# A new opening for attention followed by a max-out MoE layer: V of batches 0 and 1 by hardware queue, weights in another order, M early, nine spans of 512 tokens

## The chip, the cores and the metric

The kernel runs on one core of one Trainium2 chip. The metric is the device time of one execution in microseconds (us); the time before is the median of three runs. The core has five engines with a queue of instructions each, executed in order: PE (matmul; its weight loads are listed as PEld), DVE (VectorE), ACT (ScalarE), POOL (GpSimd) and SP (SyncE, which here only starts DMA transfers). Engines wait for each other through semaphores. SP's and ACT's transfers go through hardware queues, Pool's through a software queue.

## The reference

Block-causal attention (8 batches, 8 heads, 576 tokens, head dimension 64, blocks of 64), then a layer on its output:

```
scores = q @ k.T / 8, masked where block(query) < block(key)
attn   = softmax(scores);  x = (attn @ v), heads side by side: 4608 tokens x 512
g      = maximum(x @ w1, x @ w2)          # w1, w2: 512 x 1024
out    = g @ w_out                        # w_out: 1024 x 512, result float32
```

All inputs are fp32; the kernel computes in bf16 with fp32 sums.

## The kernel before, in words

**The algebra.** max(a, b) = max(a - b, 0) + b. So the kernel forms d = w1 - w2 (`diff_w`, lines 160 to 162, DVE), g = max(x @ d, 0) (`h_unit`, lines 202 to 221), and M = w2 @ w_out (512 x 512, `m_unit`, lines 234 to 244, from w2 transposed by `bT_unit`, lines 223 to 232). Then out = x @ M + g @ w_out (`y_unit`, lines 252 to 264): 4 matmuls with M and 8 with w_out for a tile of 128 tokens.

**Attention.** A pair is two heads of one batch; there are 32 pairs, four a batch, and a group g is two pairs (16 groups). `load_qk` (line 112) brings q and k of a group (589,824 bytes each) into one of three raw buffers; with `gated` a one-element memset on Pool stands ahead, so that SP's transfer starts no earlier than Pool reaches it. `cast` (line 126) makes bf16, `transposes` (line 346) turns it on PE and copies PSUM to qT, kT. Scores are computed transposed (keys on partitions), go through two PSUM buffers (`ps_s`, bufs=2), and `exp` (line 394, ACT) writes them to aT. `mask` (line 399, Pool memsets) clears what causality forbids. `av` (line 463) multiplies aT by V, which carries a column of ones, so that DVE can divide by the row sums (lines 485, 486) into xp. `x_out` (line 503) transposes xp on PE into xT; for groups 4 to 14 `x_dma` does it by DMA. Pairs 0 to 3 (batch 0) are written as four bursts each (`burst_p`, `burst_q1`, `burst_q2`, `burst_q3`: 768, 1024, 1024 and 384 columns), pairs from 4 on as three tiles (`tile_0` to `tile_2`). A burst or tile needs the `ps_s` buffer of the one before last, hence the end of its exp.

V comes by `load_v` (line 134): a Pool (software) DMA that casts to bf16, five chunks of up to 128 keys a batch. w1, w2 and w_out come by Pool DMAs too, w2 and w_out cast on the way: w1 and w2 in four blocks of 256 columns, w_out in two halves. w2 rests in a part of xT that later batches overwrite.

**The order of the work** is written out by hand (`manual_schedule`): each engine executes what is emitted for it in the order of the code. Matmuls of the layer are filler: `plan` (line 285) lists units (h, bT, M, y), each with the token count it needs and a cost per matmul (1.0 for 512 columns, 0.5 for M, 0.25 for bT), and `fill(n)` (line 322) emits the next ready ones up to cost n. `fill_of(g)` (line 534) shares what is ready among the groups until the next batch's tokens are done.

Lines 578 to 680 are the opening. Warm-ups (`warm_up`, line 338) are matmuls on zeros. Batch 0's bursts are interleaved with the first `diff_w`, h and bT; q and k of group 2 arrive, and the tiles of pairs 4 and 5 (`region`, lines 657 to 667) follow at once, beside h; M and the first y units come after these. From line 682 the loop over groups 3 to 15 runs regions, fills, `av_with` of the pair two back, and `pool_work` (line 541), which emits on Pool the gated loads three groups ahead, the casts of q and k two groups ahead (`cast("q", 4)` and `cast("k", 4)` at s = 5), and `load_v` of the next batch.

The layer goes by spans of tokens. `spans` (lines 71, 72) are 256, 320, then 512 each, last 448; since a span may end inside a tile of 128 tokens, `carry` (line 76) counts the tokens handed to the next span, and `h_unit` copies their g on Pool (line 207).

Of the kernel before, what the change touches and what calls it, by code (L numbers as in the profile page):

```python
# [8 lines left out]
FP32 = mybir.dt.float32  # L9
BF16 = mybir.dt.bfloat16  # L10
# [4 lines left out]
def kernel(  # L15
# [55 lines left out]
    spans = [(0, QCUT), (QCUT, S - QCUT)]  # L71
    spans += [(t0, min(SPAN, NTOK - t0)) for t0 in range(S, NTOK, SPAN)]
    NSPAN = len(spans)


    carry = [t0 % P for t0, _ in spans]
    tiles = [(carry[i] + w) // P for i, (_, w) in enumerate(spans)]
# [62 lines left out]

    w1r = moe_w1.rearrange("(c p) f -> p c f", p=P)
# [4 lines left out]
    w1_raw, w2_sb = {}, []  # L146
    for j in range(d_ff // WB):
        row, n = (1, j) if j < 3 else (3, 0)
        t0 = 3 * S - 3 * BLK + n * NDM * WB
        w2_sb.append(xT[:, row, t0:t0 + NDM * WB].rearrange("p (c f) -> p c f", c=NDM))  # L150

    def load_w(j, which=(0, 1)):
        fs = slice(j * WB, (j + 1) * WB)
        if 0 in which:
            w1_raw[j] = wraw.tile([P, NDM, WB], FP32, name="w1raw")
            nc.gpsimd.dma_start(out=w1_raw[j][:], in_=w1r[:, :, fs])
        if 1 in which:
            nc.gpsimd.dma_start(out=w2_sb[j], in_=w2r[:, :, fs])

    def diff_w(j):  # L160
        fs = slice(j * WB, (j + 1) * WB)
        nc.vector.tensor_sub(d_sb[:, :, fs], w1_raw[j][:], w2_sb[j])  # L162
# [17 lines left out]
    load_qk(2, (SP, None))  # L180
# [10 lines left out]
    for c in range(2):  # L191
        load_v(0, c)
    load_w(0, (0,))
    cast("q", 1, ((pool, 7, RPP),))
    cast("k", 1, ((pool, 0, 7),))
    load_w(0, (1,))


# [3 lines left out]
    def h_unit(i, f):  # L202
        if f == 0:
            g_tiles[i] = g_pool.tile([P, NFF, SPAN + BLK], BF16, name="g")
            if carry[i]:
                end = carry[i - 1] + spans[i - 1][1]
                nc.gpsimd.tensor_copy(  # L207
                    out=g_tiles[i][:, :, :carry[i]],
                    in_=g_tiles[i - 1][:, :, end - carry[i]:end])
        g = g_tiles[i]  # L210
        t0, w = spans[i]
        m = carry[i]
        pt = ps_m.tile([P, SPAN], FP32, name="ps_h", tag="m")
        for c in range(NDM):
            nc.tensor.matmul(  # L215
                pt[:, :w], d_sb[:, c, f * P:(f + 1) * P], xT[:, c, t0:t0 + w],
                start=(c == 0), stop=(c == NDM - 1),
            )
            if c == NDM - 1:
                nc.vector.tensor_scalar_max(g[:, f, m:m + w], pt[:, :w], 0.0)  # L220
            yield

    def bT_unit(j):
        pt = ps_m.tile([P, 2, NDM, P], BF16, name="ps_bT", tag="m")
        for i in range(2):
            for c in range(NDM):
                nc.tensor.transpose(pt[:, i, c, :], w2_sb[j][:, c, i * P:(i + 1) * P], ident[:])
                if i == 1 and c == NDM - 1:
                    (act if j % 2 else dve)(
                        out=bT_sb[:, 2 * j:2 * j + 2, :],  # L230
                        in_=pt.rearrange("p i c d -> p i (c d)"))
                yield

    def m_unit(i, c):
        ds = slice(i * WH, (i + 1) * WH)
        pt = ps_m.tile([P, WH], FP32, name="ps_M", tag="m")
        for f in range(NFF):
            nc.tensor.matmul(  # L238
                pt[:], bT_sb[:, f, c * P:(c + 1) * P], wo_sb[:, f, ds],
                start=(f == 0), stop=(f == NFF - 1),  # L240
            )
            if f == NFF - 1:
                nc.vector.tensor_copy(out=m_sb[:, c, ds], in_=pt[:])
            yield

    def y_terms(i, s):
        g = g_tiles[i]
        t0 = spans[i][0] - carry[i] + s * P
        return [(xT[:, c, t0:t0 + P], m_sb[:, c]) for c in range(NDM)] + [
            (g[:, f, s * P:(s + 1) * P], wo_sb[:, f]) for f in range(NFF)]  # L250

    def y_unit(i, s):
        t0 = spans[i][0] - carry[i] + s * P
        py = ps_m.tile([P, d_model], FP32, name="ps_y", tag="m")
        terms = y_terms(i, s)
        for n, (lhs, rhs) in enumerate(terms):
            nc.tensor.matmul(  # L257
                py[:], lhs, rhs, start=(n == 0), stop=(n == len(terms) - 1),
            )
            if n == len(terms) - 1:  # L260
                y = y_pool.tile([P, d_model], FP32, name="y")
                (dve if i < 2 else act)(out=y[:], in_=py[:])  # L262
                nc.sync.dma_start(out=out[t0:t0 + P, :], in_=y[:])
            yield

    def y_last(i, s):
        t0 = spans[i][0] - carry[i] + s * P
# [17 lines left out]
    def plan():  # L285
        def h(i, f):
            t0, w = spans[i]
            units.append((h_unit(i, f), t0 + w, w / SPAN, NDM))

        def y(i, s, last=False):  # L290
            t0, w = spans[i]
            if last:
                units.append((y_last(i, s), t0 + w, 0.333, 3 * NY))
            else:
                units.append((y_unit(i, s), t0 + w, 1.0, NY))

        for i in range(NSPAN):
            for f in range(NFF):
                h(i, f)
                if i == 0 and f % 2:  # L300
                    units.append((bT_unit(f // 2), 0, 0.25, 2 * NDM))
                if i > 2 and f % 2 == 0 and f // 2 < tiles[i - 1]:
                    y(i - 1, f // 2)
            if i == 1:
                for n in range(2 * NDM):
                    units.append((m_unit(n // NDM, n % NDM), 0, 0.5, NFF))
                for j in range(2):
                    for s in range(tiles[j]):
                        y(j, s)
        n = tiles[-1]  # L310
        for s in range(n):
            y(NSPAN - 1, s, s == n - 1)

# [88 lines left out]
    def burst(p, parts, a0):  # L402
        u = ps_s.tile([P, 2, 512], FP32, name="ps_s", tag="s")
        w = 0
        for c, q0, n in parts:
            scores(p, u, w, c, q0, n)
            w += n
        exp(p, u, w, a0)

    def burst_p(p):  # L410
        burst(p, ((0, 0, QCUT), (1, P, QCUT - P)), 0)

    def burst_q1(p):
        burst(p, ((0, QCUT, 320), (1, QCUT, 192)), 384)

    def burst_q2(p):
        burst(p, ((1, 448, P), (2, QCUT, 320), (4, 512, BLK)), 896)

    def burst_q3(p):
        burst(p, ((3, 384, 192),), 1408)  # L420

    def masks_p(p, eng=None):
        for a in (0, 256):
            mask(p, a, eng)
# [116 lines left out]
    def pool_work(s):  # L541
        g, i = divmod(s, 2)
        if s == 4:
            load_qk(4, (SP, SP), gated=True)
# [31 lines left out]
    LOW = (0, -(-QCUT // RPP))  # L576
    HIGH = (LOW[1], NP)
# [9 lines left out]
    burst_p(0)  # L587
    masks_p(0)
# [3 lines left out]
    for c in range(2, NCH):  # L592
        load_v(0, c)
    load_qk(2, (None, SP), gated=True)
    load_w(1)
    cq = transposes("q", 1, (dve, dve))
    burst_q1(0)
    ck = transposes("k", 1, (dve, dve))
    for i in range(2):
        cq((i,), LOW)  # L600
        ck((i,), LOW)
    cq((0,), HIGH, act)
    cq((1,), HIGH, act)
    warm_up(3)
    burst_p(2)
    ck((0,), HIGH, dve)
    ck((1,), HIGH, dve)
    av(0, [0, 1])
    warm_up(2)
    burst_p(3)  # L610
    av(1, [0, 1])
    masks_p(2, nc.vector)
    burst_q3(0)
    masks_p(3, nc.vector)
    burst_q2(0)
    av(2, [0, 1])
    warm_up(2)
    x_out(0, 0, 2, (act, act))
    av(3, [0, 1])
    diff_w(0)  # L620
    burst_q1(1)
    warm_up(2)
    cast("q", 2, ((pool, 0, RPP),))
    masks_q(0)
    load_w(2)
    burst_q2(1)
    x_out(1, 0, 2)
    warm_up(2)
    burst_q3(1)
    masks_q(1)  # L630
    load_w(3)
    fill(4)
    burst_q1(2)
    transposes("q", 2, (dve, act))()
    burst_q2(2)
    av(0, [2, 3, 4])
    burst_q3(2)
    masks_q(2)
    cast("k", 2, ((pool, 0, RPP),))
    load_wo(0)  # L640
    load_wo(1)
    av(1, [2, 3, 4])
    burst_q1(3)
    burst_q2(3)
    av(2, [2, 3, 4])
    transposes("k", 2, (dve, act))()
    burst_q3(3)
    masks_q(3)
    pad_keys(4)
    pad_keys(5)  # L650
    load_qk(3, (SP, SP), gated=True)
    for c in range(NCH):
        load_v(1, c)
    x_out(0, 2, NCH)
    diff_w(1)
    fill(2)
    outs = tile_0(4), tile_1(4)
    av(3, [2, 3, 4])
    region(*outs)
    fill(2)  # L660
    diff_w(2)
    fill(4)
    x_out(1, 2, NCH)
    region(tile_2(4), tile_0(5))
    diff_w(3)
    fill(6)
    region(tile_1(5), tile_2(5))
    fill(6)
    cast("q", 3, ((pool, 0, RPP),))
# [88 lines left out]
```

The softmax here doesn't subtract the row's maximum and nothing guards it: scores larger than these inputs give would overflow.

## Time and profile before

| what | us |
|---|---|
| median of three runs (258.4 to 258.81) | 258.6 |
| the profiled execution's own time | 260.0 |
| its span, first to last instruction | 258.2 |
| PE busy | 247.4 |
| ACT busy / DVE busy / POOL busy | 143.2 / 136.1 / 110.4 |
| exps of batch 0 (16 bursts) | from 8.9 to 26.0 |
| exps of pairs 4 and 5 | from 26.7 to 34.4 |
| first scores of pair 6 (group 3 starts) | 42.2 |
| x_out(2) on PE (group 4 starts) | 55.2 |
| x_out(3) on PE (group 5 starts) | 66.3 |
| last matmul ends | 255.1 |

Times within the span count from its start. A row of groups gives the line, the engine, the operation, the output and input tiles with their shapes, the count, then the busy time and the mean ns of one, then the engine's idle time just before them and what ended most of it. In rows of the timeline the first two numbers are start and duration.

### The profile page before, as it was taken

How to read it: one execution, taken by the hardware profiler on the slowest of the kernel's cores; microseconds unless marked ns; L12 is line 12 of the kernel's file. 1: busy time of each engine (PE TensorE's matmuls, PEld its weight loads, DVE VectorE, ACT ScalarE, POOL GpSimd, SP SyncE). 2: the span in 40 equal slices, each digit the busy share in tenths (PEclk: the TensorE clock that was granted, in tenths of full speed). 3: DMA queues.
4: the chain of work that ended last, by engine and by line, in shares of the span. 5: the costliest groups of instructions: out<-in, count | busy, mean ns of one | idle time of the engine just before them, and what ended most of it. 6: DMA issues, size and time to landing. Idle time of an engine off the chain costs nothing.

```text
span 258.2 us, 7195 instructions
## 1 busy us (share of the span) xinstructions
PE 247.4 (96%) x2983; PEld 139.1 (54%) x2983; DVE 136.1 (53%) x299; ACT 143.2 (55%) x200; POOL 110.4 (43%) x274
## 2 busy tenths in 40 slices
PE   7598899799999999999999999999999999999995
PEld 2346678646555555555555554546464655444444
DVE  4967986556584428451845184518550853443200
ACT  2798854476574857586757665766576431000111
POOL 1987950584637263726382638163813010000000
PEclk9999999999999999999999999999999999999999
DMA  6999999499569995998599949985977122202122
GB/s 244 316 206 307 217 251 246 156 102 253 129 162 257 144 188 135 245 154 225 114 244 143 186 145 224 168 196 141 91 109 110 44 56 80 83 0 81 43 104 99
DMA packets 71265, 41.30 MB, mean 160 GB/s; under 512 B 53568, under 2 KB 58048, under 8 KB 71232
## 3 DMA queue, kind: packets, MB, share of 16 engines
q1 hardware_dynamic: 28544, 31.27, 43.4%
q0 software_dynamic: 42272, 8.92, 39.9%
q10 hardware_dynamic: 416, 0.66, 0.7%
q8 instruction: 23, 0.38, 0.6%
q14 instruction: 10, 0.08, 0.1%
HBM read 34.60 MB, written 9.44 MB: 171 GB/s over the span
## 4 chain that ended last, share of the span: by engine, by line
PE 84%; DMA 8%; POOL 3%; ACT 2%; issue 1%; DVE 0%; SPq 0%; POOLq 0%; ACTq 0%
PE ps_y L257 36%; PE ps_h L215 22%; PE ps_o L479 10%; PE ps_s L371 8%; DMA qraw<-in_q_dram 5%; DMA kraw<-in_k_dram 3%; PE ps_qT L352 2%; PE ps_kT L352 2%; PE ps_w L341 1%; ACT aT L395 1%; PE ps_y L272 1%; PE ps_M L238 1%; POOL kn L132 1%; PE ps_s L389 1%; ACT qT L360 1%
## 5 line engine op out<-in xcount | busy, mean ns | idle before, releaser
L395 ACT ACTIVATE aT<-ps_s 128x1024 bf16<-128x1024 f32 (+2 forms) x100 | 95.8, 996 | 25.8 <-PE ps_s L371 24.2
L257 PE MATMUL ps_y<-wo_sb,g 128*128 128x512 bf16 x280 | 69.8, 379 | 0.0
L215 PE MATMUL ps_h<-xT,d_sb 128*128 128x512 bf16 (+3 forms) x320 | 69.2, 358 | 0.3 <-DVE d_sb L162 0.3
L220 DVE TENSOR_SCALAR g<-ps_h 128x512 bf16<-128x512 f32 (+3 forms) x80 | 50.7, 636 | 30.6 <-PE ps_h L215 28.8
L400 POOL MEMSET aT<- 64x128 bf16 x124 | 22.4, 200 | 81.8 <-ACT aT L395 81.2
L485 DVE RECIPROCAL rec<-ps_o 128x4 f32<-128x4 f32 (+1 forms) x64 | 12.1, 188 | 62.5 <-PE ps_o L479 61.7
L215 PEld LDWEIGHTS <-d_sb 128*128 128x128 bf16 x320 | 29.0, 98 | 29.1 <-issue 2.7
L479 PEld LDWEIGHTS <-aT 128*128 128x128 bf16 x960 | 37.2, 98 | 13.5 <-issue 0.8
L262 ACT COPY y<-ps_y 128x512 f32<-128x512 f32 x31 | 18.2, 587 | 44.5 <-PE ps_y L257 36.1
L257 PEld LDWEIGHTS <-g 128*128 128x128 bf16 x280 | 25.8, 98 | 29.8 <-issue 2.0
L479 PE MATMUL ps_o<-vv,aT 128*128 128x65 bf16 x960 | 39.8, 194 | 0.0
L257 PE MATMUL ps_y<-m_sb,xT 128*128 128x512 bf16 x140 | 38.2, 380 | 0.0
L136 POOL DMA_DIRECT2D vv<-in_v_dram x40 | 33.7, 848 | 1.6 <-issue 1.2
L371 PE MATMUL ps_s<-qT,kT 64*128 64x64 bf16 (+6 forms) x344 | 31.2, 280 | 1.6 <-ACT kT L360 0.7
L486 DVE TENSOR_TENSOR xp<-ps_o,rec 128x256 bf16<-128x256 f32 (+1 forms) x64 | 31.4, 491 | 2.2
L360 ACT COPY qT<-ps_qT 128x576 bf16<-128x576 bf16 (+1 forms) x17 | 10.3, 614 | 19.9 <-PE ps_qT L352 19.9
L132 POOL CAST qn<-qraw 128x1152 bf16<-128x1152 f32 (+1 forms) x16 | 16.9, 1058 | 9.1 <-DMA qraw<-in_q_dram 9.1
L257 PEld LDWEIGHTS <-xT 128*128 128x128 bf16 x140 | 12.2, 98 | 15.1 <-issue 3.5
L371 PEld LDWEIGHTS <-kT 64*128 64x128 bf16 x344 | 12.3, 94 | 11.0 <-issue 6.2
L132 POOL CAST kn<-kraw 128x1152 bf16<-128x1152 f32 (+1 forms) x15 | 17.1, 1140 | 1.4 <-DMA kraw<-in_k_dram 1.4
L360 ACT COPY kT<-ps_kT 128x576 bf16<-128x576 bf16 x15 | 9.6, 639 | 14.4 <-PE ps_kT L352 14.4
L207 POOL COPY g<-g 128x512 bf16<-128x512 bf16 x8 | 4.9, 614 | 20.7 <-DVE g L220 20.3
(58 smaller groups left out, 161.8 us busy)
## 6 DMA issues: line engine op xcount, KB each, us to landing
qraw<-in_q_dram SPq DMA_DIRECT2D x16, 576.0 KB, 5.0
out_dram<-y SPq DMA_DIRECT2D x35, 256.0 KB, 3.7
kraw<-in_k_dram SPq DMA_DIRECT2D x15, 576.0 KB, 5.8
vv<-in_v_dram POOLq DMA_DIRECT2D x32, 128.0 KB, 5.7
w1raw<-in_moe_w_dram POOLq DMA_DIRECT2D x4, 512.0 KB, 8.1
xT<-in_moe_w_dram POOLq DMA_DIRECT2D x4, 256.0 KB, 8.6
wo_sb<-in_moe_w_out_dram POOLq DMA_DIRECT2D x2, 512.0 KB, 10.0
kraw<-in_k_dram ACTq DMA_DIRECT2D x1, 576.0 KB, 5.6
```

The source lines that it names most:

```text
L132: copy(out=n[:, j0:j1], in_=t[:, j0:j1])
L136: nc.gpsimd.dma_start(out=vv_r[b % NV][P - rows:, c, :, :D], in_=v[b, :, c * P:c * P + rows, :].rearrange("h p d -> p h d"),)
L215: nc.tensor.matmul(pt[:, :w], d_sb[:, c, f * P:(f + 1) * P], xT[:, c, t0:t0 + w], start=(c == 0), stop=(c == NDM - 1),)
L220: nc.vector.tensor_scalar_max(g[:, f, m:m + w], pt[:, :w], 0.0)
L257: nc.tensor.matmul(py[:], lhs, rhs, start=(n == 0), stop=(n == len(terms) - 1),)
L262: (dve if i < 2 else act)(out=y[:], in_=py[:])
L360: (copy or copies[i])(out=t[:, p0 * RPP:p1 * RPP].rearrange("q (p j) -> q p j", j=RPP), in_=pts[i][:, :, p0:p1].rearrange("q j p -> q p j"),)
L371: nc.tensor.matmul(ps[:, hh, col:col + w], kT[r, k0:k0 + P], qT[r, q0:q0 + w], start=True, stop=True,)
L395: nc.scalar.activation(out=aT_r[p % NA][:, :, a0:a0 + w], in_=ps[:, :, :w], func=AF.Exp, scale=scale,)
L400: (eng or nc.gpsimd).memset(aT_r[p % NA][BLK:, :, a0:a0 + BLK], 0.0)
L479: nc.tensor.matmul(po[:, gi, hh, :], a[:, hh, a0:a0 + P], vv[:, c, h0 + 2 * hh, :], start=(mm == 0), stop=(mm == n_mm - 1),)
L486: nc.vector.tensor_mul(xp[:, :, ts[0]:ts[0] + n, p % 2].rearrange("q s t d -> q t s d"), po[:, :, :, :D], rec[:, :n].to_broadcast([P, n, 2 ...
```

## The change

1. `stage_v(b, c)` loads a chunk of V as fp32 by SP into a free part of xT, `cast_v` copies it to bf16 (Pool). Batch 0 is staged right after q and k of group 1, where before q of group 2 was loaded; batch 1 after the loads of groups 2 and 3. Batches 2 to 7 keep `load_v`.
2. w2 is loaded in two halves (behind the casts of q1 and of k1 on Pool), then w_out in two halves, then w1 in four blocks.
3. Batch 0's four pairs run pair by pair (all bursts of pair 0, then pair 1, then 2 and 3), with warm-ups inside the bursts; bT and M are planned first and fill the later bursts; h follows once batch 0 is done; the loads of q and k for groups 2, 3 and 4 are gated behind batch 0's last masks, and the tiles of pairs 4 and 5 come after most of h of span 0.
4. Spans are nine times 512 tokens; the carry is gone.
5. Some PSUM copies change engine.

```diff
-    spans = [(0, QCUT), (QCUT, S - QCUT)]
-    spans += [(t0, min(SPAN, NTOK - t0)) for t0 in range(S, NTOK, SPAN)]
-    NSPAN = len(spans)
-    carry = [t0 % P for t0, _ in spans]
-    tiles = [(carry[i] + w) // P for i, (_, w) in enumerate(spans)]
+    NSPAN = NTOK // SPAN
+    NT_SPAN = SPAN // P
...
+    def v_stage(c):
+        row, n = (0, c) if c < 3 else (2, c - 3)
+        t0 = 3 * S - 3 * BLK + n * 2 * H * D
+        return xT[:, row, t0:t0 + 2 * H * D].bitcast(FP32).rearrange("p (h d) -> p h d", h=H)
+    def stage_v(b, c):
+        rows = min(P, S - c * P)
+        nc.sync.dma_start(
+            out=v_stage(c)[P - rows:],
+            in_=v[b, :, c * P:c * P + rows, :].rearrange("h p d -> p h d"),
+        )
+    def cast_v(b, c, copy):
+        rows = min(P, S - c * P)
+        copy(out=vv_r[b % NV][P - rows:, c, :, :D], in_=v_stage(c)[P - rows:])
...
+    def load_w2(i):
+        nc.gpsimd.dma_start(out=w2_sb[i], in_=w2r[:, :, i * WC:(i + 1) * WC])
...
-    load_qk(2, (SP, None))
+    for c in range(NCH):
+        stage_v(0, c)
...
-    for c in range(2):
-        load_v(0, c)
-    load_w(0, (0,))
     cast("q", 1, ((pool, 7, RPP),))
+    load_w2(0)
     cast("k", 1, ((pool, 0, 7),))
-    load_w(0, (1,))
...
 def bT_unit:
-                    (act if j % 2 else dve)(
+                    nc.vector.tensor_copy(
 def m_unit:
-                nc.vector.tensor_copy(out=m_sb[:, c, ds], in_=pt[:])
+                (act if i else dve)(out=m_sb[:, c, ds], in_=pt[:])
 def y_unit:
-                (dve if i < 2 else act)(out=y[:], in_=py[:])
+                (dve if i < 1 else act)(out=y[:], in_=py[:])
...
 def burst(p, parts, a0, warm=0):
         u = ps_s.tile([P, 2, 512], FP32, name="ps_s", tag="s")
         w = 0
+        for _ in range(warm):
+            nc.tensor.matmul(u[:, 0], zeros[:, :P], zeros[:], start=True, stop=True)
...
 def pool_work(s):
         if s == 4:
-            load_qk(4, (SP, SP), gated=True)
+            for c in range(NCH):
+                cast_v(1, c, pool)
```

The opening after the change, from the first burst on (one line holds several statements of the code):

```
burst_p(0); load_w2(1); masks_p(0); burst_p(1); warm_up(2); masks_p(1)
for c in range(3): cast_v(0, c, pool)
load_wo(0); transposes("q", 1, (dve, dve))(); burst_q1(0); transposes("k", 1, (dve, dve))()
burst_q2(0, 2); burst_q3(0, 2); masks_q(0)
for c in range(3, NCH): cast_v(0, c, pool)
load_wo(1); load_w1(0); load_w1(1)
burst_q1(1, 2); burst_q2(1, 2); av(0, [0, 1]); burst_q3(1, 2); masks_q(1); fill(2)
burst_p(2, 1); av(0, [2, 3, 4]); burst_p(3); masks_p(2); masks_p(3); fill(2)
av(1, [0, 1]); burst_q1(2); av(1, [2, 3, 4]); burst_q2(2); x_out(0); fill(4)
burst_q3(2); masks_q(2); load_w1(2); load_w1(3); av(2, [0, 1]); burst_q1(3, 1)
av(3, [0, 1]); burst_q2(3, 1); fill(4); burst_q3(3); masks_q(3); fill(4)
for g in (2, 3): load_qk(g, (SP, SP), gated=True)
for c in range(NCH): stage_v(1, c)
load_qk(4, (SP, SP), gated=True)
av(2, [2, 3, 4]); fill(4); av(3, [2, 3, 4]); fill(4); x_out(1, 0, NCH, (act, act))
diff_w(0); fill(8); cast("q", 2, ((pool, 0, RPP),)); diff_w(1); fill(8)
cast("k", 2, ((pool, 0, RPP),)); fill(8); diff_w(2); fill(8)
transposes("q", 2, (dve, act))(); diff_w(3); fill(8); transposes("k", 2, (dve, act))()
pad_keys(4); pad_keys(5); fill(5); region(tile_0(4), tile_1(4)); fill(6)
region(tile_2(4), tile_0(5)); fill(6); cast("q", 3, ((pool, 0, RPP),))
region(tile_1(5), tile_2(5)); fill(6); cast("k", 3, ((pool, 0, RPP),))
```

What follows (the rest of group 2, and the loop over groups 3 to 15) is unchanged in its text.

## Prediction, made before the changed kernel was run

> **What bounds the kernel now.** I read the page first, then the busy time by stretches, then the groups, then the timeline of the first 70 us. The page:
>
> ```profile
> span 258.2 us, 7195 instructions
> ...
> PE 247.4 (96%) x2983; PEld 139.1 (54%) x2983; DVE 136.1 (53%) x299; ACT 143.2 (55%) x200; POOL 110.4 (43%) x274
> ...
> PE   7598899799999999999999999999999999999995
> ...
> ACT  2798854476574857586757665766576431000111
> POOL 1987950584637263726382638163813010000000
> ...
> DMA  6999999499569995998599949985977122202122
> ```
>
> PE is full from about slice 9 (55 us) on; only the opening and the tail have room. I cut the opening where the work changes: first transposes (7.0), end of batch 0's exps (26.1), first scores of pair 6 (42.2), start of group 5 (66.3). The columns are the window, its length, and the busy time of PE, PEld, DVE, ACT, POOL.
>
> ```profile
> 7.00:26.10 19.10, 15.75 (x323) 9.94 (x323) 14.89 (x38) 16.08 (x25) 16.57 (x30) 1.00 1.43 273
> 26.10:42.20 16.10, 15.34 (x209) 11.49 (x208) 14.03 (x29) 9.57 (x12) 9.93 (x28) 1.00 1.66 217
> 42.20:66.30 24.10, 22.48 (x348) 14.55 (x347) 13.25 (x31) 15.11 (x20) 12.19 (x33) 1.00 0.87 182
> 66.30:240.00 173.70, 173.70 (x2001) 93.10 (x2001) 88.07 (x182) 96.85 (x135) 69.90 (x181) 1.00 0.77 143
> ```
>
> Busy PE time hides slow pace, so I price PE work by the distance between starts of successive matmuls in the full stretch: 216 ns for 512 columns (h, y), 109 for 256 (M), 56 for bT, 29 for av, 14.5 for a transpose; 0.85 us for a pair's scores. At these prices the useful work, warm-ups not counted, is 8.7 us from 7.0 to 26.1, 15.5 up to 42.2, 22.2 up to 66.3. So the three stretches lose 10.4, 0.6 and 1.9 us (together 12.9); later almost nothing. **The question is whether the new order loses less than 12.9 us before the same state is reached.**
>
> The other prices, from the groups:
>
> ```profile
> L395 ACT ACTIVATE aT<-ps_s 128x1024 bf16<-128x1024 f32 (+2 forms) x100 | 95.8, 996 | 25.8 <-PE ps_s L371 24.2
> L136 POOL DMA_DIRECT2D vv<-in_v_dram x40 | 33.7, 848 | 1.6 <-issue 1.2
> L132 POOL CAST qn<-qraw 128x1152 bf16<-128x1152 f32 (+1 forms) x16 | 16.9, 1058 | 9.1 <-DMA qraw<-in_q_dram 9.1
> ```
>
> And the one long stall after 42 us, PE behind Pool's cast of q4, itself waiting for its load:
>
> ```profile
> 46.18 1.15 POOL L132 CAST qn<-qraw 128x1152 bf16<-128x1152 f32 x1 [3.89 <-DMA qraw<-in_q_dram]
> 47.38 0.44 PE L352 MATMUL ps_qT<-ident,qn 64*128 64x64 bf16 x18 [1.61 <-POOL qn L132]
> ```
>
> **The Trainium skill.** "TensorE: Matmul & The Clock Gate", Back-to-back issue gap, gives N/2.4 + 2.5 ns: 216 ns for 512 columns, as the trace has it. "DMA: Bandwidth & Descriptors", SWDGE vs HWDGE vs iDMA: a transfer that casts must come from GpSimd; so V by a hardware queue lands as fp32 and needs a cast. Same page, Why small descriptors are slow: a 256-byte piece takes 11 cycles instead of 8. "GPSIMD Engine Reference", Engine selection: one-input copies run near line rate; here 256 columns took 0.41 us and 1152 took 1.14, so 0.2 us + 0.81 ns a column.
>
> **The change, part by part.**
>
> *V by hardware queue.* Ten software issues (V of batches 0, 1), about 0.85 us each, 8.4 us, leave Pool's queue. Ten casts of 512 columns come: 0.2 + 512 x 0.81 ns = 0.62 us each, 6.2 us. Loading: by software a chunk is 1024 packets, and the packet records show some 1100 of them per us: 0.95 us. By hardware no row shows it: if it keeps the 2048-byte pace (84 ns a packet, 16 engines) 0.67 us; at the 256-byte packets' mean of the later transposes (32 ns) 2.0 us; the skill's 11/8 on the weights' 374 GB/s gives an estimate of 0.96. I take 0.96: chunks land from 10.5 to about 14.5 us, sharing with w2. A gain against software isn't excluded, but k1, ahead in that queue, lands at 9.3 in any case.
>
> *Weights.* Order w2, w_out, w1, 2.1 MB each; now 128 packets of 4096 bytes (0.52 MB of w1) take about 1.4 us, so 5.7 us for each. Behind V that fills the DMA engines to about 30 us: w2 by 18 to 19, w_out 24, w1 30. q2 (gated behind batch 0's last masks, 27 us) lands near 32, k2 33, q3, k3 36, V of batch 1 41, q4, k4 44. SP's eleven issues from 27 on take 0.4 to 1.0 us each and are out before the first y store queues behind them (46 us). None of the loads is late for its user below except perhaps w2's first half (bT at 15.5, landing 15 to 16.5: 0 to 1 us).
>
> *Batch 0's bursts.* Each waits for the PSUM buffer of the burst before last; where two warm-ups stand ahead, release to next exp costs 0.05 + 0.43 + 0.38 + 0.04 = 0.9 us, hidden behind a 1.02 us exp, not behind one of 0.5. Exps start at 8.94 as now; they are 4 x (0.78 + 1.02 + 1.02 + 0.5) = 13.3 us. Gaps: 0.3 up to q3 of pair 0; 0.4 each behind the short q3s and where av, bT or M stand between (six places, 2.3); 1.6 where x_out(0) waits for DVE and two bT units follow it. Sum 4.2: end at 8.94 + 13.3 + 4.2 = 26.4, against 26.03 now. Pool just keeps up: masks to 11.6, three casts to 13.5, w_out's issue, masks, two casts to 16.0; av(0) of the late tiles wants them at 16.5. The four masks moved from DVE to Pool (0.8 us) and the 13 burst warm-ups (against 13 before) lie in waits: nothing; were av(0) late, each us would be one of the end.
>
> *M, then h, ahead of pairs 4 and 5.* After 26.4, PE ends M1 at 26.7 and then has av (1.8), M2 to M7 (48 x 109 ns, 5.2), x_out(1) (0.5), 29 matmuls of h (6.3) and q2's and k2's transposes (0.7): 41.2, with latencies 41.4. Copies that change engine (x_out(1) and half of M to ACT, bT and x_out(0) to DVE) fall where that engine waits; y copies stay 4 on DVE. PE is full, loses nothing. At 42.0 useful work done is 24.5 of 35, lost 10.5; before had lost 11.0 by 42.2. **A draw so far.** But pairs 4 and 5 had their six exps between 26.7 and 34.4 before; now ACT stands without exps from 26.4 to 41.8. And of batch 0's 120 filler units 87 are planned before group 3, instead of 56 of 124.
>
> *Groups 2 to 4 without filler.* From 41.8 ACT owes pairs 4 to 9: 18 exps x 0.98 + 6 x 0.27 + 6 copies of qT/kT x 0.64 = 23.1 us; PE only 21.0 (scores 5.1, av 3.6, transposes 1.6, x_out 1.0, 45 units 9.7). Walking on: pairs 4, 5 keep ACT to 48.4. Pool meanwhile does q3's cast, masks, k3's cast to 49.95, and then the five casts of V, **3.1 us that its queue puts ahead of pad_keys(6, 7) and of q4's and k4's casts**: pads to 54.1, q4 55.3, k4 56.4. Transposes of k3 at 50.3, copies to 51.0, first exp of pair 6 at 51.5 (ACT without work for some 2.5 us). Its third tile is issued behind q4's transposes: PE waits 54.0 to 55.3, and ACT from 53.5 to 55.7. Then each region costs ACT's 2.7 to 3 us plus small gaps: group 4 starts at 59.8 (8 or 9 units of filler), its q5 cast is awaited 0.2 us, group 5 starts at 68.8. PE did 21.0 of 26.8: lost 5.8.
>
> *Nine spans.* Same columns: 32 x (109 + 136 + 189) ns = 13.9 us become 64 x 216 = 13.8. Eight Pool copies (4.9 us) go, on nobody's path. But at group 5 span 0 covers 512 tokens instead of 576: four matmuls more remain, 0.9 us.
>
> **Sum.** 68.8 - 66.3 + 0.9 = +3.4 us; or by losses: 10.5 + 5.8 against 12.9. After group 5 PE is full in both, so all of it reaches the end: span 258.2 to 261.6. The profiled run gave 260.0 around a span of 258.2; the runs' median is 258.6. On the median: **262.0 us**. A difference under 0.2% (0.5 us) can't be told from none.
>
> **Rivals.**
> *Faster.* If Pool's casts and the wait for buffers leave ACT no gap from 41.8, pair 9's last exp ends at 41.8 + 23.1 = 64.9, and group 5 starts some 2 us (two exps) earlier, near 63; PE's own 21.0 says the same, 63.0. Then 63.0 - 66.3 + 0.9 = -2.4: 256.2. It decides for faster as soon as group 5 starts before 65.4. For it: 8.4 us of issues leave Pool, ACT's copies for q1, k1 leave the opening. Against it: Pool's chain above, and PE's two-tile regions. Halfway it is a draw.
> *V late.* At 2.0 us a chunk beside w2, the last chunks land near 20; Pool stands in cast_v with the masks and weight issues queued behind it, PE at av(0) with the next scores behind it: 4 us more, 266. Against it: w1's large pieces kept the full pace.
> *My forecast*, ACT-bound groups 3 and 4: 260 to 264.
>
> **Chances.** Forecast and its neighbours (slower, up to 264) 0.57; V or weights late 0.17; draw 0.06; faster 0.20. So faster 0.20, same 0.06, slower 0.74. Leaving out a tenth at each end gives 257.0 to 266.0.
>
> **What would show it.** Right: exps of batch 0 end within 1 us of 26.4; no exp until 41 to 43; PE's idle time, now in slices 1 to 8, appears between 47 and 69, released by Pool's qn and by ACT's aT; PE full from 69. Wrong: pair 6's first exp before 49, or group 5 (second PE x_out of batch 1) before 65.4. Idle at ps_o released by Pool's vv before 20 would be the late V.

## The result, and the profile after

The changed kernel takes **282.8 us** (median of four runs, 282.18 to 283.5), against 258.6 (258.4 to 258.81): a ratio of 1.094, 95% interval 1.091 to 1.097. Slower, as predicted, but by 24.2 us where 3.4 were forecast, and far outside the range. Medians and intervals in this document leave out runs that took over 1.5% longer than the fastest of the same kernel (one each of e2, e11 and e12 below). The profiled execution's span is 280.6 us. Its page:

```profile
span 280.6 us, 7079 instructions
...
PE 251.3 (90%) x2916; PEld 139.0 (50%) x2953; DVE 134.6 (48%) x279; ACT 142.9 (51%) x200; POOL 101.5 (36%) x269
...
PE   8759930989877999999999999999999999999995
...
ACT  3744401247788658566774775675758541101111
POOL 1645330016797372446427453725363110000000
PEclk9995995899999999999999999999999999999999
DMA  7999798101599699779789974998699332201123
```

In slices of 7 us, PE has a 3 in the sixth and a 0 in the seventh, counted from 1 (35 to 49 us); ACT has 0 and 1 there, Pool 3 and 0. The DMA row falls to 1, 0 and 1 in the eighth to tenth. The clock row has holes, where the kernel before has:

```profile
PEclk9999999999999999999999999999999999999999
```

Cut at the same events as before (first transposes, end of batch 0's exps, first scores of pair 6, start of group 5; columns as before, then granted clock, DMA share and GB/s):

```profile
7.00:31.80 24.80, 19.79 (x288) 12.23 (x289) 13.19 (x28) 14.00 (x18) 13.06 (x30) 0.86 1.07 212
31.80:70.40 38.60, 25.54 (x273) 14.44 (x276) 16.94 (x25) 11.39 (x18) 8.84 (x25) 0.87 0.48 149
70.40:85.70 15.30, 12.80 (x280) 8.86 (x286) 9.48 (x24) 12.64 (x17) 12.44 (x31) 1.00 0.84 192
85.70:260.00 174.30, 170.21 (x1969) 92.37 (x1993) 88.92 (x183) 99.04 (x138) 66.08 (x177) 1.00 0.78 144
```

Most is lost in the second stretch: 38.6 us where the kernel before took 16.1, with 13 us without PE and a clock of 0.87. The first is 5.7 us longer than before; the third is 8.8 us shorter, since more of the filler now lies ahead of it. The waits of the first 75 us name the loss (who waits for whom; sum, count, longest):

```profile
...
ACT xT L522 <- DMA xT<-in_v_dram: 16.2, 1, 16.2
...
PE ps_M L242 <- ACT xT L522: 11.0, 1, 11.0
...
POOL vv L150 <- DMA xT<-in_v_dram: 5.1, 3, 2.6
...
PE ps_o L479 <- POOL vv L150: 3.0, 2, 2.4
```

The first two are one event, in the timeline:

```profile
34.30 9.85 SPq L143 DMA_DIRECT2D xT<-in_v_dram  x5
...
47.93 0.69 ACT L522 COPY xT<-ps_xe 128x640 bf16<-128x640 bf16 x1 [16.18 <-DMA xT<-in_v_dram]
48.52 0.59 ACT L523 COPY xT<-ps_xo 128x512 bf16<-128x512 bf16 x1
48.67 3.23 PE L242 MATMUL ps_M<-wo_sb,bT_sb 128*128 128x256 bf16 x16 [11.00 <-ACT xT L522]
```

`x_out(1)`, the last tokens of batch 0, copies PSUM to xT on ACT. The copy waits until 47.9 for transfers of **V of batch 1**, which it doesn't read; PE, needing the PSUM buffers that the copies free, stands for 11.0 us behind it. Then even M runs at half pace: 16 matmuls in 3.23 us, where 109 ns each makes 1.74.

The last two are the late V of batch 0, on Pool and PE:

```profile
15.58 0.61 POOL L150 CAST vv<-xT 128x512 bf16<-128x512 f32 x1 [2.65 <-DMA xT<-in_v_dram]
...
19.46 0.62 POOL L150 CAST vv<-xT 128x512 bf16<-128x512 f32 x1 [2.06 <-DMA xT<-in_v_dram]
...
20.13 0.43 PE L479 MATMUL ps_o<-vv,aT 128*128 128x65 bf16 x9 [2.40 <-POOL vv L150]
```

### The profile page after: what moved, and what is told of

Its sections match the earlier page's. It is cut to its first block, busy times and chain, and to the rows that moved or that the text cites. A ratio compares the mean times of both kernels' runs of the same rounds, so it can differ in the third digit from the quotient of the medians.

```text
span 280.6 us, 7079 instructions
## 1 busy us (share of the span) xinstructions
PE 251.3 (90%) x2916; PEld 139.0 (50%) x2953; DVE 134.6 (48%) x279; ACT 142.9 (51%) x200; POOL 101.5 (36%) x269
## 4 chain that ended last, share of the span: by engine, by line
PE 76%; SPq 6%; DMA 5%; ACT 4%; DVE 3%; issue 3%; POOL 2%; POOLq 0%; ACTq 0%
PE ps_y L261 31%; PE ps_h L218 21%; PE ps_o L479 10%; PE ps_s L369 6%; SPq L143 6%; DMA xT<-in_v_dram 5%; ACT aT L393 3%; PE ps_M L242 2%; PE ps_qT L350 2%; PE ps_kT L350 1%; PE ps_y L276 1%; DVE d_sb L172 1%; PE ps_bT L231 1%; DVE g L223 1%; POOL vv L131 1%
## 5 line engine op out<-in xcount | busy, mean ns | idle before, releaser
L393 ACT ACTIVATE aT<-ps_s 128x1024 bf16<-128x1024 f32 (+2 forms) x100 | 95.9, 996 | 31.6 <-PE ps_s L369 31.0
L223 DVE TENSOR_SCALAR g<-ps_h 128x512 bf16<-128x512 f32 x72 | 49.5, 689 | 44.3 <-PE ps_h L218 43.5
L218 PE MATMUL ps_h<-xT,d_sb 128*128 128x512 bf16 x273 | 66.8, 379 | 2.6 <-DVE g L223 1.2
L479 PEld LDWEIGHTS <-aT 128*128 128x128 bf16 x960 | 38.4, 99 | 17.2 <-issue 4.2
L479 PE MATMUL ps_o<-vv,aT 128*128 128x65 bf16 x960 | 41.0, 195 | 3.3 <-POOL vv L150 3.0
L218 PEld LDWEIGHTS <-d_sb 128*128 128x128 bf16 x288 | 26.3, 98 | 31.5 <-issue 3.8
L266 ACT COPY y<-ps_y 128x512 f32<-128x512 f32 x31 | 18.2, 587 | 45.1 <-PE ps_y L261 32.9
L261 PE MATMUL ps_y<-m_sb,xT 128*128 128x512 bf16 x126 | 36.1, 380 | 1.3 <-issue 0.9
L369 PE MATMUL ps_s<-qT,kT 64*128 64x128 bf16 (+6 forms) x344 | 32.4, 284 | 4.2 <-ACT aT L451 1.6
L131 POOL DMA_DIRECT2D vv<-in_v_dram x30 | 25.1, 842 | 0.5
L261 PEld LDWEIGHTS <-xT 128*128 128x128 bf16 x140 | 12.2, 98 | 15.5 <-issue 4.0
L358 ACT COPY qT<-ps_qT 128x576 bf16<-128x576 bf16 x15 | 9.6, 639 | 19.1 <-PE ps_qT L350 19.1
L242 PE MATMUL ps_M<-wo_sb,bT_sb 128*128 128x256 bf16 x64 | 9.3, 302 | 11.0 <-ACT xT L522 11.0
```

What stands on the lines that cost most here:

```text
L131: nc.gpsimd.dma_start(out=vv_r[b % NV][P - rows:, c, :, :D], in_=v[b, :, c * P:c * P + rows, :].rearrange("h p d -> p h d"),)
L218: nc.tensor.matmul(pt[:], d_sb[:, c, f * P:(f + 1) * P], xT[:, c, t0:t0 + SPAN], start=(c == 0), stop=(c == NDM - 1),)
L223: nc.vector.tensor_scalar_max(g[:, f], pt[:], 0.0)
L261: nc.tensor.matmul(py[:], lhs, rhs, start=(n == 0), stop=(n == len(terms) - 1),)
L266: (dve if i < 1 else act)(out=y[:], in_=py[:])
L358: (copy or copies[i])(out=t[:, p0 * RPP:p1 * RPP].rearrange("q (p j) -> q p j", j=RPP), in_=pts[i][:, :, p0:p1].rearrange("q j p -> q p j"),)
```

## The experiments

Two theories stood behind the first runs. **A:** the 24 us are two transfers that arrive late for someone: the copies of `x_out(1)` wait for staged data that only lies *between* the rows which they write, and V of batch 0 loses the DMA engines to w2. **B:** the price lies in the new order itself or in staging V. In later runs A and B are as each expectation says. Fifteen kernels were run, each beside the kernel before, whose median lay between 258.7 and 259.0 in these runs. The key events (us within the profiled span):

| kernel | exps of batch 0 end | first exp of pair 4 | first exp of pair 6 | group 5 starts | last matmul starts | median | ratio to before, 95% |
|---|---|---|---|---|---|---|---|
| before | 26.0 | 26.7 | 42.7 | 66.3 | 254.9 | 258.6 | 1 |
| predicted | 26.4 | 41.8 | 51.5 | 68.8 | | 262.0 | |
| after | 31.8 | 60.9 | 70.9 | 85.7 | 277.0 | 282.8 | 1.091 to 1.097 |
| e1_rows | 31.9 | 48.6 | 58.5 | 73.7 | 265.0 | 271.9 | 1.046 to 1.058 |
| e2_rows_w2late | 27.6 | 44.3 | 54.2 | 70.7 | 263.7 | 267.5 | 1.028 to 1.042 |
| e3_rows_v0soft | 32.9 | 49.6 | 59.6 | 74.7 | 267.7 | 273.6 | 1.051 to 1.062 |
| e4_rows_vsoft | 31.6 | 48.3 | 58.2 | 74.4 | 265.8 | 271.5 | 1.047 to 1.052 |
| e5_pairs45_early | 27.4 | 38.5 | 57.4 | 73.4 | 264.8 | 269.7 | 1.040 to 1.044 |
| e6_vsoft_btlate | 30.6 | 47.3 | 57.3 | 72.0 | 263.3 | 268.8 | 1.032 to 1.044 |
| e7_rows_w2small | 31.6 | 48.3 | 58.3 | 73.4 | 264.8 | 271.7 | 1.043 to 1.056 |
| e8_h_later | 27.1 | 41.9 | 53.2 | 70.2 | 260.8 | 266.5 | 1.027 to 1.031 |
| e9_relu_act | 27.2 | 42.2 | 54.6 | 71.3 | 261.5 | 266.7 | 1.024 to 1.032 |
| e10_keep_clock | 27.1 | 43.8 | 54.3 | 73.7 | 264.9 | 270.4 | 1.039 to 1.048 |
| e11_before_q4_first | 26.0 | 26.7 | 42.7 | 65.7 | 254.3 | 260.2 | 1.004 to 1.008 |
| e12_q2_early | 27.3 | 42.6 | 55.6 | 72.6 | 262.9 | 268.5 | 1.026 to 1.040 |
| e13_half_weights | 28.3 | 39.5 | 50.8 | 67.8 | 258.1 | 263.9 | 1.017 to 1.022 |
| e15_split_copies | 31.1 | 47.8 | 57.8 | 72.6 | 263.9 | 270.0 | 1.040 to 1.048 |
| e16_q2_first | 32.8 | 39.6 | 54.5 | 71.9 | 262.4 | 267.5 | 1.030 to 1.037 |

**e1_rows: V staged elsewhere.** Same loads, issues and casts; the last two chunks go to row 1, and behind row 3's batch 0 tokens, in place of row 2.

```diff
-        row, n = (0, c) if c < 3 else (2, c - 3)
+        row, n = (0, c) if c < 3 else (2 * c - 5, 2)
```

> Chunks 3 and 4 of the staged V lie in the free ends of rows 1 and 3 of xT instead of row 2; no transfer, queue or order is changed. Theory A: x_out(1)'s two copies on ACT wait for the staged V of batch 1 only because a row between the two that they write holds it, not for any byte of theirs; the copies start at about 36 us, PE's idle stretch from 37.6 to 48.4 us goes (10.8 us), and the half clock after it too (some 1.6 us): about 270 us. Theory B: the wait is only put down to that transfer and another one ends as late (k of group 2, the queue of SP): 282 to 283 us, the copies still at about 48 us.

271.9 us: 10.9 of the 24.2 are gone, as A said. The same copy in its timeline starts 12 us earlier, and waits for PE's transposes alone:

```profile
35.97 0.69 ACT L522 COPY xT<-ps_xe 128x640 bf16<-128x640 bf16 x1 [4.11 <-PE ps_xe L517]
```

**e15_split_copies: the same wait removed the other way.** V stays where the change put it; each copy over rows 2 and 3 is split in two.

```diff
-        copies[0](out=dst[:, :, :, 0], in_=pe[:])
-        copies[1](out=dst[:, :, :n_odd, 1], in_=po[:])
+        for s in range(2):
+            copies[0](out=dst[:, s, :, 0], in_=pe[:, s])
+            copies[1](out=dst[:, s, :n_odd, 1], in_=po[:, s])
```

> The changed kernel with the staged V where it is, but each PSUM copy of x_out written as two, one for each row of xT (four copies instead of two for each x_out). Theory A (the wait in x_out(1) is for the stretch of addresses from the first to the last element of one copy, which takes in the staged V between its two rows): the wait goes as in e1_rows, 271 to 272 us. Theory B (the copies share something real with the staged V of batch 1): 282 to 283 us, copies at 48 us.

```profile
35.21 0.42 ACT L523 COPY xT<-ps_xe 128x320 bf16<-128x320 bf16 x1 [4.11 <-PE ps_xe L517]
```

270.0 us, the wait is gone. Together these two show the cause. The instructions in the traces agree: in the changed kernel this copy waits for PE and two DMA semaphores, in both experiments for PE alone. Bytes in common can't explain it, since the staging is the same in e15 and the bytes written too. What fits all three kernels is that a copy over rows 2 and 3 is held to depend on everything from its first to its last element, and that the two staged chunks in row 2, past batch 0's tokens, lie between.

**e2_rows_w2late: w2 behind V.** On e1; w2's issues move behind the third cast of V, w_out behind the fifth; the first bT units follow one or two bursts later.

```diff
-    load_w2(0)
...
     burst_p(0)
-    load_w2(1)
...
     for c in range(3): cast_v(0, c, pool)
+    load_w2(0); load_w2(1)
-    load_wo(0)
...
     for c in range(3, NCH): cast_v(0, c, pool)
+    load_wo(0)
...
-    fill(2)
     burst_p(2, 1)
...
     burst_q1(2)
+    fill(2)
```

> As e1_rows, and both halves of w2 are issued behind V's third cast instead of among V's transfers, w_out behind the fifth cast; two of the bT fills move later by one or two bursts. Theory A: the last chunks of V of batch 0 are late (19.4 and 20.4 us) because each of their 256-byte packets takes turns with a 1024-byte packet of w2; now they land by 14.5 us, PE's stall from 17.7 to 21.2 us goes, batch 0's exps end near 27 instead of 31.7 us and the clock stays full: about 4 us less than e1_rows, 266 us. Theory B: a chunk by hardware takes its 2 us and more because of its issue on SP (2.4 and 3.3 us were seen): they still land near 19 us, and the time is that of e1_rows or above it, since w2 comes later.

267.5 us, another 4.4. V's packets (256 bytes) that ended in each us, beside w2's (1024 bytes), from the packet records:

```
us          9    10   11   12   13   14    15   16   17   18   19
after, V    900  546  99   150  210  1004  441  115  147  330  64
after, w2   0    45   148  151  147  21    102  158  151  92   9
e2, V       888  848  849  835  467  31    0    0    0    0    0
e2, w2      0    0    0    0    0    0     27   173  203  193  197
```

Alone, V moves 830 to 1000 packets a us; in e2 the chunks land 1.2 to 1.4 us apart (predicted 0.96). Beside w2 the two sorts end in about equal numbers (459 and 446 in us 11 to 13, 262 and 309 in us 16 and 17), and the small ones get about a sixth of their pace. "DMA: Bandwidth & Descriptors" in the Trainium skill, Queues, rings and completion order, says that an engine takes turns between its queues, a group of descriptors from each. The records agree in that both queues end about as many packets; how many make up one turn they don't show. That turns count packets and not bytes is what I had not worked out. So the third to fifth chunks land at 15.5 to 20.4, in e2 at 12.8 to 15.5. In e2 Pool's third cast starts at 12.8, and PE waits for w2 instead:

```profile
12.83 0.61 POOL L150 CAST vv<-xT 128x512 bf16<-128x512 f32 x1 [0.58 <-DMA xT<-in_v_dram]
...
19.33 0.62 PE L230 MATMUL ps_bT<-ident,xT 128*128 128x128 bf16 x8 [1.90 <-DMA xT<-in_moe_w_dram]
```

**e7_rows_w2small: w2 in quarters.** On e1; packets of 512 bytes against V's 256.

```diff
-        nc.gpsimd.dma_start(out=w2_sb[i], in_=w2r[:, :, i * WC:(i + 1) * WC])
+        for n in range(0, WC, WB):
+            nc.gpsimd.dma_start(
+                out=w2_sb[i][:, :, n:n + WB], in_=w2r[:, :, i * WC + n:i * WC + n + WB])
```

> As e1_rows, but each half of w2 is loaded as two blocks of 256 columns, so that its packets are 512 bytes instead of 1024. Theory A (packets of the two queues take turns one by one): a turn of w2 lasts about 60 instead of 100 ns, V's packets come more often, its last chunk lands near 19 instead of 20.9 us, 1 to 2 us less than e1_rows. Theory B (V's share is set by bytes or by its own issue): landing and time as e1_rows, 272 us.

V's last two casts start some 2 us earlier than in e1, as turn-taking says, yet the time is e1's: 271.7. PE's clock seems to have taken it back; no run separates the two. In e7 PE runs at half clock from 22.4 to 29.2, where bT and bursts lie (16 bT matmuls took 1.89 us; in e1 1.07); in e1 that stretch was 19.0 to 25.8, half of it waiting. e1 to e2 therefore holds both: V's lateness and a half-clock stretch in the opening that e2 doesn't have.

**e3_rows_v0soft, e4_rows_vsoft, e6_vsoft_btlate: V by software again.** e3 is e1 with batch 0's V by `load_v`; e4 is e3 with batch 1's too; e6 is e4 with bT one or two bursts later, as in e2.

```diff
-    for c in range(NCH):
-        stage_v(0, c)
...
+    for c in range(2): load_v(0, c)
     cast("k", 1, ((pool, 0, 7),))
+    for c in range(2, NCH): load_v(0, c)
+    load_w2(0)
...
-        stage_v(1, c)
+        load_v(1, c)
```

> As e1_rows, but V of batch 0 comes by Pool's software queue with the cast on the way, as before the change (two chunks ahead of k1's cast, three behind it, w2 behind them); batch 1 stays staged. Theory A (the late V of batch 0 costs the opening 4 to 5 us): all chunks land by 16 us, exps of batch 0 end near 27 us, 266 us. Theory B (the opening's exps are late for the order of the bursts, not for V): no change against e1_rows within 1 us.

> As e3_rows_v0soft, and V of batch 1 too by the software queue, so that nothing of the staging is left; Pool issues five transfers behind the gated memsets and makes no casts in group 3. Theory A (the prediction's step: 3.1 us of casts on Pool ahead of pad_keys(6, 7) and of q4's and k4's casts hold PE and ACT in group 3): 1 to 2 us less than e3_rows_v0soft. Theory B: ACT is the bound of groups 3 and 4 anyway, or q4 lands later: within 0.5 us of it.

> As e4_rows_vsoft (all of V by the software queue), and the first two bT fills one or two bursts later, as in e2_rows_w2late. Theory A: e3 and e4 gained nothing in the opening because w2, now behind V in one queue, landed near 20 us and PE stood at the first bT unit as long as it had stood for V; with bT later the stall goes, batch 0's exps end near 28 us: 267 to 268 us, as e2_rows_w2late, so that V's queue itself is worth nothing. Theory B (the software transfers of V are slower or hold Pool's masks): still 271.

e3, 273.6: no gain over e1, w2 now stands behind V in the software queue and PE waits 4.3 us at bT. e4, 271.5: 2.1 less, the size that A gave to Pool's five casts for batch 1; but the profiles don't put it there. From pair 4 to pair 6 both take 10.0 us, and in e2 PE's longest wait for Pool's qn in these groups is 0.35 us. e4 is ahead by 1.3 us at the end of batch 0 already, before these casts, and by 0.3 at group 5. From pair 10's first exp to the end e3 takes 194.1 us and e4 192.3; e3's profile has a stretch at half clock there (77.4 to 80.8). So A's number was met and its reason not shown. e6, 268.8: bT's wait shrinks to 2.9 us, and the time is 1.3 above e2's, with runs from 267.2 to 270.6 against e2's 266.0 to 269.2. So **staging V by the hardware queue is by itself neither gain nor loss** that these runs could tell; what counts is when w2 arrives.

**e5_pairs45_early: pairs 4 and 5 ahead of h.** On e2; q2 and k2 loaded earlier, their tiles between batch 0's last av and h, `x_out(1)`'s copies on DVE, and 27 units of filler in one piece after them.

```diff
+    load_qk(2, (SP, SP), gated=True)
...
-    fill(5)
+    x_out(1, 0, NCH, (dve, dve))
+    fill(4)
     region(tile_0(4), tile_1(4))
-    fill(6)
+    diff_w(0)
+    fill(8)
     region(tile_2(4), tile_0(5))
...
+    fill(27)
```

> As e2_rows_w2late, but q and k of group 2 are loaded behind the masks of pair 3's first burst, and the tiles of pairs 4 and 5 stand right behind batch 0, between M and h, with 27 units of filler behind them; the sum of the filler in the opening is the same. Theory A (the prediction's step: ACT without exps from the end of batch 0 to pair 4, 27.6 to 44.3 us in e2_rows_w2late, is what makes groups 2 to 4 ACT-bound): first exp of pair 4 near 31 us, of pair 6 near 47 instead of 54, group 5 starts near 67 instead of 70.7 us, about 4 us less: 264 us. Theory B (PE's own work and the shortage of filler bound these groups whatever ACT's order): within 1 us of 268.

269.7, 2.2 more than e2. Pair 4's exps start 5.8 us earlier, and pair 6's 3.2 later: the filler that stood before pair 4 now stands before pair 6. Not a gain.

**e8_h_later, e9_relu_act.** e8 is e2 with the last three of five `fill(8)` before pair 4 taken out (their units come later); e9 is e8 with the maxima of span 0's eight h units on ACT.

```diff
     cast("k", 2, ((pool, 0, RPP),))
-    fill(8)
     diff_w(2)
-    fill(8)
     transposes("q", 2, (dve, act))()
     diff_w(3)
-    fill(8)
     transposes("k", 2, (dve, act))()
...
+                if i == 0:
+                    nc.scalar.activation(out=g[:, f], in_=pt[:], func=AF.Relu)
+                else:
+                    nc.vector.tensor_scalar_max(g[:, f], pt[:], 0.0)
```

> As e2_rows_w2late, but three of the eight-unit fills (h) ahead of pairs 4 and 5 are left to the fills of groups 2 to 4, so 63 of 120 units are planned ahead of group 3's fills instead of 87. Theory A: pair 4's first exp comes 5 us earlier, near 39 us, and the 24 units spread over groups 2 to 4 hide behind ACT: 2 to 3 us less than e2_rows_w2late. Theory B: within 1 us of it.

> As e8_h_later, but the maxima of span 0's eight h units are taken by ACT (Relu) instead of DVE (0.69 us each). Theory A: between x_out(1) and pair 4, DVE is the bound, with four diff_w of 1.22 us and the maxima and copies of qT, kT in one queue (4.0 of 4 us busy); with ACT idle there, pair 4's first exp comes about 1 us earlier and the time falls by about 1 us, 265.5 us. Theory B: q and k of group 2, landing near 36 us, set pair 4's start: within 0.5 us of e8_h_later; if Relu made ACT load another table between exps, 2 us or more slower.

e8, 266.5: 1.0 less than e2 and inside its spread, so no gain that these runs could tell. Pair 4 starts only 2.3 us earlier although three times eight units (5.2 us) are out of its way; q2 and k2 aren't there sooner. e9, 266.7: nothing more, so with the units out of the way DVE isn't what holds pair 4.

**e12_q2_early, e16_q2_first, e13_half_weights: is it the load?** e12 is e8 with q2 and k2 gated six bursts (6.3 us) earlier, ahead of w1's last two blocks. e16 is e5 with q2 loaded ahead of V of batch 0 and k2 right behind it, and without the 27 units in one piece. e13 is e12 with 2.6 of the 6.3 MB of weights left out: it loads only the first block of w1 and the first half of w_out, and y reads bT in the place of w_out, so that its output is not the reference's.

```diff
+    load_qk(2, (SP, SP), gated=True)
...
-    for g in (2, 3):
-        load_qk(g, (SP, SP), gated=True)
+    load_qk(3, (SP, SP), gated=True)
```

```diff
+        if j:
+            w1_raw[j] = w1_raw[0]
+            return
...
-        nc.gpsimd.dma_start(out=wo_sb[:, :, ds], in_=wor[:, :, ds])
+        if i == 0:
+            nc.gpsimd.dma_start(out=wo_sb[:, :, :WH], in_=wor[:, :, :WH])
```

> As e8_h_later, but q and k of group 2 are loaded behind the masks of pair 3's first burst instead of behind batch 0's last masks. In e8_h_later PE waits 2.2 and 1.1 us for the casts of q2 and k2 (35 to 38.5 us) and falls to half clock behind that. Theory A: they land by 30 us, pair 4's first exp comes at 37 to 38 instead of 41.9 us, 2 to 3 us less, 264 us. Theory B: q2 and k2 take DMA time from w_out and w1, so M waits instead: within 1 us of e8_h_later.

> As e5_pairs45_early, with q of group 2 loaded ahead of the staged V of batch 0 and k of group 2 right behind it, both casts on Pool behind pair 3's first masks, and without the 27 units of filler in one piece (they go to the fills of groups 2 to 4). Theory A (what is left over the kernel before is that pairs 4 and 5 come late because their q and k are loaded behind the weights): pair 4's first exp comes at 29 to 32 us, group 5 starts near 67 us, 259 to 262 us. Theory B (V of batch 0 and w2 behind q2 now delay batch 0 by as much, or PE has lost the work that filled its waits): 265 us or more.

> As e12_q2_early, but only the first of four blocks of w1 and the first half of w_out are loaded and used in place of the others (the y units take bT in place of w_out): 2.6 MB less to load, some 7 us of the DMA engines, with all instructions on PE, DVE and ACT kept in number and size; the output is not the reference's. Theory A: the opening of all these versions is bound by what has to be loaded; with q2 and k2 early the weights come late instead (PE waits 2.5 us at h, 1.9 us at pair 4's scores), and with 7 us less these waits go: 3 to 5 us less than e12_q2_early, 264 to 265 us. Theory B: Pool's or DVE's queue holds h and pair 4: within 1 us of 268.7.

e12, 268.5, gains nothing over e8: w1's last block lands at 39.9 instead of 34.6. DVE's `diff_w` waits for w1's blocks, the copies of qT and kT queue behind it, and PE behind those:

```profile
37.68 1.23 DVE L172 TENSOR_TENSOR d_sb<-w1raw,xT 128x1024 bf16<-128x1024 f32 x1 [1.10 <-DMA w1raw<-in_moe_w_dram]
...
39.63 0.38 PE L217 MATMUL ps_h<-xT,d_sb 128*128 128x512 bf16 x1 [2.48 <-DVE qT L357]
...
41.90 1.03 PE L368 MATMUL ps_s<-qT,kT 64*128 64x512 bf16 x6 [1.89 <-DVE kT L357]
```

e16, 267.5: against e12, pair 4 starts 3 us sooner and batch 0 ends 5.6 us later. e13, 263.9: 4.6 us less than e12, with pair 6 at 50.8, near the predicted 51.5. Pool issues four transfers fewer in e13, but batch 0 ends there 1.0 us later than in e12, so those issues show no gain. Not all of the 4.6 us is loading as such: e12's profile has half clock from 40.7 to 47.6, behind the waits shown, and e13's has none; e12's one run at a mean clock of 0.994 took 265.05. The three kernels agree with an opening bound by loading time, directly and by the clock that falls behind the waits: what is loaded sooner makes something else late.

**e10_keep_clock: warm-ups in groups 3 to 5,** on e2, in PE's gaps.

```diff
+        if g < 6:
+            warm_up(4)
...
+            if g < 5:
+                warm_up(3)
```

> As e2_rows_w2late, with warm-up matmuls ahead of the scores of groups 3 to 5 (four ahead of a group's first region, three ahead of each further one in groups 3 and 4), where PE waits for ACT. Theory A: the two stretches of 3.4 us at half clock (63 to 66 and 73 to 77 us in the profile) come from PE's low share there and cost 1 to 2 us each where PE has work; with the warm-ups the clock stays full: 2 us less, 266 to 266.5 us, and a narrower spread of runs. Theory B: the stretches fall into waits and cost nothing, and the warm-ups delay scores: 268 to 270 us.

The clock stays full, and all six runs lie within 0.16 us, but it costs: 270.4. Pair 10's first exp comes 2.8 us later than in e2; from there to the end it takes 1.6 us less (192.5 against 194.1).

**e11_before_q4_first: the kernel before, q4 and k4 loaded ahead of V of batch 1,** to shorten its one long stall.

```diff
-            load_qk(4, (SP, SP), gated=True)
+            for c in range(NCH):
+                load_v(1, c)
...
-    for c in range(NCH):
-        load_v(1, c)
+    load_qk(4, (SP, SP), gated=True)
```

> The kernel before, with one move: q and k of group 4 are loaded right behind those of group 3, and V of batch 1 (software queue, five transfers) in their old place in pool_work(4). In the kernel before, PE stood from 45.8 to 47.4 us for q4's cast, whose load landed at 46.1 behind V. Theory A: q4 lands near 40 us, the stall goes, V of batch 1 still lands before its first use at 57 us: 1.0 to 1.6 us less than before, 257.2 us. Theory B: V's five issues on Pool (4.2 us) now stand ahead of q4's cast, which ends no earlier than 45 us: within 0.3 us of before.

Its profile shows the stall halved, 1.61 to 0.86 us, and a span of 257.6; yet its median over 21 runs is 260.2, 0.4% to 0.8% slower than the kernel before. Why isn't known. Nothing tried beats the kernel before.

## Why the prediction was right and wrong

**Slower: right, but for 3.4 of 24.2 us at most.** By difference of medians, 10.9 us are the wait for staged V at `x_out(1)` and the half clock behind it (after to e1), 4.4 the turns of V with w2 and the half clock that came with them (e1 to e2), and 8.9 remain.

**`x_out(1)` "0.5 us": the step that failed.** It was priced as PE work plus a change of engine. Staging put a transfer into a row that its copies span, ahead of it in the order of the code, and the new wait was not looked for; nor was the question asked "who else writes this tile?". The landing was off as well: V of batch 1 at 43.4 to 47.8, where 41 was said. SP held its five issues for 9.85 us, where the sum had under 1 each, but that isn't what made it late: k3, ahead of it, landed at 42.7 where 36 was said, and V's last chunk 5.1 us behind that, as predicted. The loads came late because batch 0 ended late (first of them issued at 32.2, where 27 was said), and the weights ran behind their sum too, in e2 as well: w1's last block at 35.0 where 30 was said, q2 at 36.2 for 32. "None of the loads is late for its user" fell here.

**V of batch 0, "land from 10.5 to about 14.5", sharing with w2.** The price of a chunk alone was near (1.2 for 0.96). The sharing was not worked out: beside w2 the last two land at 19.3 and 20.4. The rival *V late* described this (PE at av(0) behind Pool's casts, 4 us); it had 0.17 and I argued against it from w1's pace, whose packets of 4096 bytes are the large ones in such turns. Batch 0's exps ended at 31.8, not 26.4.

**Pairs 4 and 5, "PE is full, loses nothing".** In e2, with both waits gone, it is 16.7 us from the end of batch 0 to pair 4's first exp, where 15.4 were predicted. DVE's queue was unpriced: `diff_w` (four at 1.22 us) and the maxima (0.69 each) stand ahead of the copies of qT and kT, and PE shows gaps of 0.4 and 0.7 for DVE at 39.5 and 42.5. e8, without this filler, is then held by q2 and k2.

**Groups 2 to 4: right in sum, in part by luck, and not in the part that is Pool's.** Pair 4 to group 5 was predicted at 27.0 us; e2 has 26.5, the changed kernel 24.8; pair 4 to pair 6 is 10.0 in both (predicted 9.7). Pool's five casts are in e2 where they were put, after k3's cast:

```profile
51.97 2.98 POOL L150 CAST vv<-xT 128x512 bf16<-128x512 f32 x5
...
55.56 1.15 POOL L127 CAST qn<-qraw 128x1152 bf16<-128x1152 f32 x1
```

```profile
56.77 0.44 PE L349 MATMUL ps_qT<-ident,qn 64*128 64x64 bf16 x18 [0.35 <-POOL qn L127]
...
63.40 0.61 PE L368 MATMUL ps_s<-qT,kT 64*128 64x64 bf16 x4 [0.82 <-ACT aT L450]
```

They took 2.98 us (3.1 predicted), but PE waits 0.35 for q4's cast where 1.3 was said: pair 6 itself is 2.7 us later, and the filler between covers it. What PE waits for in these groups is ACT, 2.9 us from 44 to 76. The rival *Faster* needed these groups in 21.2 us; of what keeps them longer, the runs show waits for ACT, and not Pool.

**After group 5, "PE is full in both".** Nearly. From pair 10's first exp to the end of the span: 191.1 before, 192.5 in e1, e10 and after. Of these 1.4, 0.9 is the predicted delay of nine spans; no run did the spans alone. e2's 194.1 holds one 3.4 us stretch at half clock more.

**The remaining 8.9.** By e2's profile (span 267.3, predicted 261.6): +1.2 at the end of batch 0, +1.3 up to pair 4, -0.5 in groups 2 to 4, +1.6 at group 5's beginning, where scores wait for `ps_s` behind ACT, +2.1 after that. The profiled run had two stretches at half clock; e2's one run at a mean clock of 0.999 had a span of 264.0, only 2.4 over the predicted one. So some 3 of these 5.7 us go with the clock, which the prediction did not price. The loads have a part in the rest (e13). The last 5 us over the kernel before, which stay even in e13, were not taken apart; the order of batch 0's bursts and the PSUM copies that change engine had no run of their own either.

## What to carry to other kernels

When a transfer is put into a spare part of a tile that others write, list every later writer of that tile, and check whether its first-to-last extent encloses the new data; if so, place the data outside or split the writer. When a load of small packets is to run beside a load of large ones, price it by equal numbers of packets from each, not by bytes. And when the opening is bound by loading, moving one load forward only chooses who waits.

## What the runs showed of the hardware

**Half clock where PE was thinly used.** The profile of the kernel before has no stretch at half clock. Most variants of the changed one have, in lengths of 3.41 us or a multiple: after 20.7 to 27.5 and 41.2 to 51.4, e1 19.0 to 25.8, e8 38.1 to 41.5. "TensorE: Matmul & The Clock Gate" in the Trainium skill, The HAM clock gate, gives a free-running window of 3413 ns, which these lengths agree with, and half clock after an idle window. Here a window need not be idle: in e2 no gap of PE from 44 to 80 us was longer than 0.82 us, and the clock fell for 63.0 to 66.4 and 73.2 to 76.6, where PE was thinly used (windows as above):

```profile
60.00:64.00 4.00, 2.28 (x46) 0.99 (x40) 2.05 (x5) 3.61 (x6) 3.02 (x9) 0.87 0.95 175
64.00:68.00 4.00, 3.54 (x62) 2.53 (x64) 2.09 (x6) 1.78 (x3) 3.99 (x7) 0.70 1.10 205
72.00:76.00 4.00, 2.85 (x11) 1.07 (x12) 0.32 (x1) 3.03 (x4) 3.22 (x9) 0.65 0.61 68
```

In the first row PE is busy 2.28 of 4 us and the clock falls at 63.0; in the second it is at half for 2.4 of 4 us. All 17 profiles can be cut into windows of 3.413 us from their first moment at full clock. The clock stayed full after each of the 1223 full-clock windows with PE recorded as busy for over 63%, and fell after each of the 12 with under 52%; of the 19 between, it fell after 6. So between these shares PE's use of a window doesn't settle it.

The times of runs follow the clock: e2's four took 266.0 us at a mean clock of 0.999, 267.5 at 0.994, and 269.2 and 270.3 at 0.987; e9's two at 1.000 took 265.4 and 265.5, its two at 0.987 267.4. With fillers in the gaps (e10) the clock stayed at 0.998 or more and the spread was gone.

**Issues that take long.** In the changed kernel a hardware-queue issue of a V chunk held SP for 0.6 to 3.9 us, the second and third of the five longest (2.4 to 3.9); in e2 one took 6.5. Its issues of q or k took 0.38 to 0.57 us in the first 50 us (later two took 1.0 and 1.07). Three of the long ones end 0.2 to 0.7 us before the k loaded ahead lands (9.02 and 9.29, 38.90 and 39.59, 42.45 and 42.68), as if the queue had no room before; no run tests this. What stands behind on SP waits that long.
